# The inverse transform over 47 rows as one matrix of 96 x 94, in groups of 376 tokens

## The chip, the cores and the metric

The kernel runs on one core of one Trainium2 chip. The metric is the device time of one execution in microseconds; less is better. The engines are named as in the profile: PE is the matrix engine (PEld its weight loads), DVE, ACT and POOL work on vectors, SP issues transfers, as ACT's queue does too.

## The reference

The input x has 8 batches of 3008 rows and 256 columns, float32. The first stage goes to the frequency domain along the rows, multiplies by a complex matrix, adds a complex bias, shrinks both parts towards zero and goes back. The second is a layer pair with 256, 2048 and 256 columns on all 24,064 rows, whose weights arrive as float64.

```python
X = np.fft.rfft(x, axis=1)
Yr = Xr @ w_r - Xi @ w_i + b_r
Yi = Xr @ w_i + Xi @ w_r + b_i
Yr = np.sign(Yr) * np.maximum(np.abs(Yr) - lam, 0.0)      # Yi likewise, lam = 0.01
y = np.fft.irfft(Yr + 1j * Yi, n=3008, axis=1)
h = y.reshape(24064, 256) @ w_in
out = np.maximum(0.01 * h, h) @ w_out
```

## The kernel before

**The transform.** 3008 is 47 x 64, and the transform along the rows is done as one of 47 (index n1, frequency k1) and one of 64 (index n2, frequency k2), with the rows reordered on the host so that no factors stand between the two. As the data are real, 24 of the 47 frequencies k1 are enough. For each batch, `fwd` does the part over n1 (matrices fa), `mid` does the part over n2 (fb), the projection by w_r and w_i with bias and threshold, and the way back over k2 (gb). Between them the data lie in DRAM, in u_dram and v_dram. `mid` writes v_dram in the order (part, k1, n2, column), with part 0 the real and part 1 the imaginary one.

**The inverse over k1** is the last step and the one that is changed. v_dram has 65 places for n2, read as 5 groups of 13 (`NG`, `NS`); place 64 is padding, which `mid` fills with zeros (L334 to L336). A set is one s out of 13, with its five n2 (four for the last s). `_pairs` puts two sets together, over the border of a batch where need be: 52 pairs, most with 470 tokens. `v_load` (L478 and its neighbours) loads for each part a tile vin with 120 partitions (24 k1 x 5 groups). `inverse` runs for each half `eh` of the 256 columns: four matmuls (L499) with a slice of vin as the 120 x 128 weights and the matrix ga of 120 x 128 as the moving operand, so that the model dimension comes to lie on the partitions. The real part gives the even half of a cosine series and the imaginary part the odd half, 24 rows each. L502 (ACT) copies the odd half out of PSUM, L503 (DVE) adds for rows 0 to 23, L505 (DVE) subtracts for rows 46 down to 24, and L512 (ACT) copies the result from y into one or two chunks yc.

**The layer pair** works on 47 chunks of 512 tokens. `forms` splits a chunk into high and low fp32r halves (yh, yl) and makes the sums of a Strassen-like scheme of seven products (`forms` L524, L525 and L543 to L547). For each of eight steps q of a chunk, `moe_a` and `moe_b` do seven products of 256 columns, three matmuls each (L94, weights win); ACT and DVE add them up and apply the leaky activation (L594 to L613), `halves` splits the result into gh and gl (L577, L579), and `moe_o` multiplies by wout, 12 matmuls of 512 columns in a step (L626).

**The order.** A planner interleaves everything: while the steps of chunk ci run, `tokens(ci + 1)` advances twice in a step, 16 times in a chunk: one yield, the `v_load` of all groups whose first token lies in chunk ci + 1 (`due`), three yields, one yield for each half of each such group (`inverse`), then six yields of `forms`. `fwd` and `mid` of later batches are streams that advance in proportion. `read` says at which chunk a batch's v_dram is first needed. PSUM has two banks under the tag psf, which `inverse` shares with `fwd`, `mid` and the projection.

**Placement.** The function `placed` gives a tile some unused elements before it (`skip`) and, in the pool sb, after it (`rest`).

Of the kernel before, what the change touches and what calls it, by code (L numbers as in the profile page):

```python
# [8 lines left out]
F32 = mybir.dt.float32  # L9
# [8 lines left out]

N1, N2, NK1 = 47, 64, 24
NG, NS = 5, 13  # L20
P = 128
PA = NK1 * NG
LAMBDA = 0.01
SLOPE = 0.01

# [5 lines left out]
def spectral_mlp_kernel(  # L31
# [16 lines left out]
    nc = tc.nc  # L48
    NB = x.shape[0]
    D = w_r.shape[0]  # L50
    DF = w_in.shape[1]
    NF = DF // P
    NH = D // P
    NPAIR = NK1 // 2
    NQ = NF // 2
    NT, HT = 512, 256
    NV = 2 * NG * N1
    CS = 512
    LAG = 2
    PAUSE = 10 * CS  # L60
# [4 lines left out]
    const = ctx.enter_context(tc.tile_pool(name="const", bufs=1))  # L65
    sb = ctx.enter_context(tc.tile_pool(name="sb", bufs=2))
    dram = ctx.enter_context(tc.tile_pool(name="dram", bufs=2, space=bass.MemoryType.DRAM))
    ps = ctx.enter_context(tc.tile_pool(name="ps", bufs=1, space=bass.MemoryType.PSUM))
    sync, act, dve, pool = nc.sync, nc.scalar, nc.vector, nc.gpsimd

    def bank(tag, bufs):
        return ps.tile([P, 512], F32, name=tag, tag=tag, bufs=bufs)

# [26 lines left out]
    consts = {}  # L100
# [6 lines left out]
    def placed(pool, shape, dtype, name, skip=0, rest=0, **where):  # L107

        n = 1
        for k in shape[1:]:  # L110
            n *= k
        axes = " ".join("abcd"[:len(shape) - 1])
        t = pool.tile([shape[0], skip + n + rest], dtype, name=name, **where)[:, skip:skip + n]
        return t.rearrange(f"p ({axes}) -> p {axes}", **dict(zip("abcd", shape[1:])))
# [4 lines left out]
            for p, k in zip(("hi", "lo"), PLACE.get(name, ((0, 0), (0, 0)))))  # L119
        return consts[name]  # L120

    def load_plain(name, src, shape, skip):
        consts[name] = placed(const, shape, F32, name, skip)
        sync.dma_start(consts[name], src)

    def split_consts():
        for name in ("wr", "wd", "wn", "gb", "fa0", "fa1"):
            w = consts[name + "32"][0]
            hi, lo = pair(name, list(w.shape))
            act.copy(hi, w)  # L130
            dve.tensor_sub(lo, w, hi.bitcast(F32))

    def load_weights():

        w = sb.tile([P, 3 * NH * D + P], F32, name="w32", tag="yl")
        r, d, n = (w[:, k * NH * D:(k + 1) * NH * D].rearrange("p (a f) -> p a f", a=NH) for k in range(3))
        i = sb.tile([P, NH, D], F32, name="w_i", tag="yt", bufs=1)
        for t, src in ((r, w_r), (i, w_i)):
# [88 lines left out]
    v_dram = {}  # L227

    reads, written, turned, turning, thresholded = [], [], [], [], []
# [99 lines left out]

    def mid(b):  # L330
        ud = u_dram[b]
        vd = dram.tile([2, NK1, NG * NS, D], F32, name="v_dram", tag="v_dram")
        v_dram[b] = vd
        zero = sb.tile([2 * NK1, D], F32, name="zero", tag="kc")  # L334
        pool.memset(zero, 0.0)
        act.dma_start(vd.rearrange("c k n d -> (c k) n d")[:, N2, :], zero)  # L336
        fbt = consts["fb"]
        u_t, e_t, z_t = {}, {}, {}
        if b == 0:
# [89 lines left out]
        def stage_g(j):  # L429
            pg = bank("psh", 4) if b < 1 else bank("psf", 2)  # L430
            last = products(pg, [(consts["gb" if b else "gb32"], tuple(flat(z) for z in z_t.pop(j)))])
            if b == 0:
                turning.append(last)
            v = sb.tile([P, 2, D], F32, name="v", tag="v" if b else "y")
            act.copy(flat(v), pg)
            for c in range(2):
                act.dma_start(vd[c, 2 * j:2 * j + 2, :N2, :].rearrange("k n d -> n k d"), v[c * N2:(c + 1) * N2])

        for j in range(2):
            load(j)  # L440
# [24 lines left out]


    pairs = _pairs(NB)
    p0 = [sum(N1 * sum(n for _, _, n in c) for c in pairs[:i]) for i in range(len(pairs) + 1)]
    nch = p0[-1] // NT
    y_t, v_t, f_t, h_t, g_t, o_t = {}, {}, {}, {}, {}, {}  # L470

    def v_load(pi):
        vin = sb.tile([PA, 2, 2, D], F32, name="vin", tag="vin")
        (b, s, _), (b1, _, _) = pairs[pi]
        for c in range(2):
            if b == b1:
                vv = v_dram[b].rearrange("c k (g s) d -> c (k g) s d", g=NG)
                ld = sync.dma_start(vin[:, c, :, :], vv[c, :, s:s + 2, :])  # L478
                if pi < 2:
                    reads.append(ld)  # L480
                continue
            for i, (b_, s_, _) in enumerate(pairs[pi]):
                vv = v_dram[b_].rearrange("c k (g s) d -> c (k g) s d", g=NG)
                sync.dma_start(vin[:, c, i, :], vv[c, :, s_, :])
        v_t[pi] = vin

    def inverse(pi, eh):


        (_, _, n0), (_, _, n1) = pairs[pi]  # L490
        m = n0 + n1
        ne, n = m * NK1, m * N1
        vin = v_t[pi]
        py = bank("psf", 2)
        s = slice(eh * P, (eh + 1) * P)
        for c in range(2):
            for i in range(2):
                o = c * ne + i * n0 * NK1
                nc.tensor.matmul(py[:, o:o + P], vin[:, c, i, s], consts["ga"][:, c, :], start=True, stop=True)  # L499
        odd = sb.tile([P, 2 * NG * NK1], F32, name="odd", tag="odd", bufs=1)[:, :ne]  # L500
        y = sb.tile([P, NT], F32, name="y", tag="y")
        act.copy(odd, py[:, ne:2 * ne])  # L502
        dve.tensor_add(y[:, :ne], py[:, :ne], odd)  # L503
        ev, ov = (t.rearrange("p (m k) -> p m k", k=NK1)[:, :, 1:] for t in (py[:, :ne], odd))
        dve.tensor_sub(y[:, ne:n].rearrange("p (m k) -> p m k", m=m), ev, ov)  # L505
        lo = p0[pi]
        while lo < p0[pi + 1]:
            ci = lo // NT
            hi = min((ci + 1) * NT, p0[pi + 1])
            if ci not in f_t:  # L510
                f_t[ci] = sb.tile([P, NH, NT], F32, name="yc", tag="yc")
            act.copy(f_t[ci][:, eh, lo - ci * NT:hi - ci * NT], y[:, lo - p0[pi]:hi - p0[pi]])  # L512
            lo = hi

    def forms(ci):
# [100 lines left out]
    def moe_o(ci, q, eh):  # L616
# [19 lines left out]

    due = [[p for p in range(len(pairs)) if p0[p] // NT == ci] for ci in range(nch)]
    read = [
        max(0, min(p0[p] // NT for p, c in enumerate(pairs) if any(x[0] == b for x in c)) - 1) + 1 / (2 * NQ)
        for b in range(NB)  # L640
    ]

# [82 lines left out]
    convert_win(0)  # L725
    with tc.issue_after(turned[0].ins):
        split_consts()
    m0 = Stream(mid(0), MID)
    m0.to(0.001)
    bias = const.tile([P, 2, D], F32, name="bias")  # L730
    with tc.issue_after(reads[3].ins):
        for r, src in enumerate((b_r, b_i)):
            sync.dma_start(bias[:, r, :], src.unsqueeze(0).broadcast_to([P, D]))
    for c in range(2, 4):
        load_win(c, (sync, sync), reads[3])
    with tc.issue_after(reads[3].ins):
        load_plain("ga", ga, [PA, 2, P], 72)
    fp = Stream(fwd(1), FWD)
    with tc.issue_after(turned[0].ins):
        convert_win(1)  # L740
# [13 lines left out]
    for p in due[0]:  # L754
        v_load(p)
# [46 lines left out]
def _constants():  # L802

    import numpy as np

    n = N1 * N2

    def angles(m, rows, cols):
        j = (rows[:, None] * cols[None, :]) % m
        c, s = np.cos(2 * np.pi * j / m), np.sin(2 * np.pi * j / m)  # L810
        s[(2 * j) % m == 0] = 0.0
        return c, s

    _, half = _sequence()
    co, si = angles(N1, np.arange(NK1), np.arange(NK1))
    weight = np.where(np.arange(NK1) == 0, 1.0, 2.0)[:, None] / n
    one = np.eye(NG)
    fa = np.stack([np.kron(co, one), np.kron(-si, one)])
    ga = np.zeros((NK1, NG, 2, P))
    for c, m in enumerate((co * weight, -si * weight)):  # L820
        ga[:, :, c, :PA] = np.einsum("kn,gh->kghn", m, one).reshape(NK1, NG, PA)
    co, si = angles(N2, np.arange(N2), np.arange(N2))
    fb = np.zeros((2, N2, NK1 + 1, N2))
    fb[0, :, 0], fb[1, :, 0] = co, si
    fb[0, :, 1:] = -si[:, None, :] * half
    fb[1, :, 1:] = co[:, None, :] * half
    gb = np.block([[co, si], [-si, co]])
    f = np.float32
    return {
        "fa": fa.astype(f),  # L830
        "fb": fb.reshape(P, NK1 + 1, N2).astype(f),
        "gb": gb.astype(f),
        "ga": ga.reshape(PA, 2, P).astype(f),
        "sg": np.concatenate([
            np.concatenate([np.ones_like(half.T), half.T]),
            half.reshape(NK1 // 2, 2 * N2).T,
        ], axis=1).astype(f),
    }


def _pairs(nb):

    sets = [(b, s, NG if (NG - 1) * NS + s < N2 else NG - 1) for b in range(nb) for s in range(NS)]
    assert len(sets) % 2 == 0
    return [sets[i:i + 2] for i in range(0, len(sets), 2)]


def _tokens(nb):

    import numpy as np  # L850

    order, _ = _sequence()
    cols = []
    for c in _pairs(nb):
        n2 = [(b, NS * g + s) for b, s, n in c for g in range(n)]
        for rows in (range(NK1), range(N1 - 1, NK1 - 1, -1)):
            cols += [b * N1 * N2 + order[i, j] for b, j in n2 for i in rows]
    return np.array(cols)


# [29 lines left out]
```

## Time and profile before

| | us |
|---|---|
| median of three runs | 2549.17 |
| lowest and highest | 2546.06, 2553.24 |
| the profiled execution | 2546.58 |
| its span, first to last instruction | 2544.8 |

The page lists first the busy time of each engine over the span. The chain that ended last is followed back from the last instruction to what released each step. A group of instructions stands in one line: line of the code, engine, operation, output and inputs by the names of the program, shape and count; then busy time, mean ns of one, and the idle time of the engine before them with what ended it. Matmuls overlap, so the mean duration of one is longer than the distance from one to the next.

### The profile page before, as it was taken

The page shows a single profiled execution, that of the slowest core. Times are in us where ns is not written, and L with a number is a line of the kernel's source. Part 1 is how long each engine was busy: PE and PEld are TensorE (multiplying, and loading weights), DVE is VectorE, ACT ScalarE, POOL GpSimd, SP SyncE. Part 2 cuts the span into 40 slices and gives each one's busy share as a digit, 9 for nine tenths or more (in the row PEclk, how much of TensorE's full clock was granted, in tenths as well). Part 3 has the DMA queues.
Part 4 walks back from the last instruction along what each step waited for, and adds up shares of the span by engine and source line. Part 5 has one row for each costly group of instructions (what it writes and reads, how often), then busy time and mean ns, then how long its engine had stood idle before and what let it go on. Part 6 is the DMA issues. An engine that isn't in the chain of part 4 may idle for free.

```text
span 2544.8 us, 42449 instructions
## 1 busy us (share of the span) xinstructions
PE 2502.0 (98%) x16204; PEld 2251.4 (88%) x16204; DVE 1880.5 (74%) x3460; ACT 1675.4 (66%) x3151; POOL 119.2 (5%) x96
## 2 busy tenths in 40 slices
PE   6999999999999999999999999999999999999999
PEld 4689889999899998999989999899998998999998
DVE  7787777777877778777787677877768777666675
ACT  4777766677667765677656777567765676666564
POOL 0001000000000000000000000000000000000000
PEclk8999999999999999999999999999999999999999
DMA  8631132111321114211141111412114111100000
GB/s 269 179 94 50 43 93 86 42 50 45 105 68 46 50 37 113 59 49 50 42 114 54 50 50 38 118 54 57 39 38 130 50 54 42 45 21 29 9 17 17
DMA packets 119904, 165.12 MB, mean 65 GB/s; under 512 B 13597, under 2 KB 69909, under 8 KB 119701
## 3 DMA queue, kind: packets, MB, share of 16 engines
q1 hardware_dynamic: 79112, 115.54, 14.8%
q10 hardware_dynamic: 40589, 46.87, 7.2%
q8 instruction: 128, 2.10, 0.3%
q14 instruction: 75, 0.61, 0.1%
HBM read 86.60 MB, written 75.76 MB: 64 GB/s over the span
## 4 chain that ended last, share of the span: by engine, by line
PE 91%; DMA 3%; DVE 2%; ACT 2%; issue 1%; SPq 0%; ACTq 0%; DVEq 0%
PE pso L626 39%; PE psh L94 34%; PE psf L80 11%; PE psf L499 3%; PE psf L361 3%; DMA xin<-x_dram 1%; PE psh L80 1%; DMA u<-u_dram 1%; DMA v_dram<-v 1%; DVE gl L579 0%; DMA win_raw<-w_in_dram 0%; ACT zf L417 0%; DMA vin<-v_dram 0%; ACT zf L413 0%; PE psh L361 0%
## 5 line engine op out<-in xcount | busy, mean ns | idle before, releaser
L94 PE MATMUL psh<-yh,win_hi 128*128 128x256 f32 (+1 forms) x2608 | 736.5, 283 | 2.4 <-DVE gf L610 2.4
L94 PE MATMUL psh<-yl,win_hi 128*128 128x256 f32 (+1 forms) x2608 | 728.7, 280 | 0.0
L94 PE MATMUL psh<-yh,win_lo 128*128 128x256 f32 (+1 forms) x2608 | 726.0, 280 | 0.0
L579 DVE TENSOR_TENSOR gl<-gf,gh 128x1024 fp32r<-128x1024 f32 x376 | 461.0, 1226 | 307.1 <-ACT gh L577 297.9
L626 PE MATMUL pso<-gh,wout_hi 128*128 128x512 f32 x1504 | 590.5, 393 | 1.1 <-ACT gh L577 1.1
L626 PE MATMUL pso<-gl,wout_hi 128*128 128x512 f32 x1504 | 589.9, 392 | 1.1 <-DVE gl L579 1.1
L626 PE MATMUL pso<-gh,wout_lo 128*128 128x512 f32 x1504 | 589.3, 392 | 0.0
L94 PEld LDWEIGHTS psh<-yh,win_hi 128*128 128x128 f32 x2608 | 489.2, 188 | 19.5 <-DVE gf L610 4.8
L94 PEld LDWEIGHTS psh<-yl,win_hi 128*128 128x128 f32 x2608 | 490.5, 188 | 16.2 <-issue 0.5
L94 PEld LDWEIGHTS psh<-yh,win_lo 128*128 128x128 f32 x2608 | 489.4, 188 | 2.0
L577 ACT CAST gh<-gf 128x1024 fp32r<-128x1024 f32 x376 | 394.9, 1050 | 42.5 <-PE pso L626 31.0
L613 ACT ACTIVATE gf<-gf 128x768 f32<-128x768 f32 x368 | 311.8, 847 | 155.5 <-DVE gf L610 143.8
L626 PEld LDWEIGHTS pso<-gl,wout_hi 128*128 128x128 f32 x1504 | 282.8, 188 | 60.0 <-DVE gl L579 2.2
L626 PEld LDWEIGHTS pso<-gh,wout_hi 128*128 128x128 f32 x1504 | 283.1, 188 | 46.8 <-ACT gh L577 1.9
L626 PEld LDWEIGHTS pso<-gh,wout_lo 128*128 128x128 f32 x1504 | 282.8, 188 | 45.9 <-issue 0.2
L612 ACT ACTIVATE gf<-psh 128x256 f32<-128x256 f32 x368 | 141.7, 385 | 227.8 <-PE psh L94 219.0
L610 DVE TENSOR_TENSOR gf<-psh,u 128x512 f32<-128x512 f32 x368 | 252.1, 685 | 27.1 <-PE psh L94 25.6
L594 ACT COPY p<-psh 128x256 f32<-128x256 f32 x368 | 136.8, 372 | 153.0 <-PE psh L94 145.4
L399 POOL TENSOR_TENSOR kb<-bias,kc 128x512 f32<-128x512 f32 x84 | 116.6, 1389 | 2056.2 <-ACT kc L397 1820.9
L595 DVE TENSOR_TENSOR u<-psh,p 128x256 f32<-128x256 f32 x368 | 154.3, 419 | 70.7 <-ACT p L594 69.4
L597 DVE TENSOR_TENSOR gf<-psh,u 128x256 f32<-128x256 f32 x368 | 154.5, 420 | 29.3 <-PE psh L94 15.2
L598 DVE TENSOR_TENSOR gf<-psh,gf 128x256 f32<-128x256 f32 x368 | 154.3, 419 | 5.5
(128 smaller groups left out, 3158.9 us busy)
## 6 DMA issues: line engine op xcount, KB each, us to landing
u<-u_dram SPq DMA_DIRECT2D x192, 128.0 KB, 2.7
v_dram<-v ACTq DMA_DIRECT2D x192, 128.0 KB, 2.4
out_dram<-ob SPq DMA_DIRECT2D x94, 256.0 KB, 2.0
vin<-v_dram SPq DMA_DIRECT2D x96, 240.0 KB, 3.5
xin<-x_dram SPq DMA_DIRECT2D x90, 240.0 KB, 3.0
u_dram<-xin ACTq DMA_DIRECT2D x72, 240.0 KB, 2.4
u_dram<-xin SPq DMA_DIRECT2D x24, 240.0 KB, 4.3
raw<-w_out_dram SPq DMA_DIRECT2D x8, 512.0 KB, 4.4
```

Of the source, the lines that this page charges most:

```text
L80: last = nc.tensor.matmul(dst, a, b, start=(i == 0), stop=(i == len(terms) - 1))
L94: mlp[:] = [nc.tensor.matmul(dst, a, b, start=start and i == 0, stop=i == 2, skip_group_check=True)]
L577: cp = act.copy(gh, g)
L579: parted[:] = [cp, dve.tensor_sub(gl, g, gh.bitcast(F32))]
L594: act.copy(p1, b1[:, lo])
L595: dve.tensor_add(u2, b1[:, hi], p1)
L597: dve.tensor_add(g[:, 3], b2[:, hi], u2)
L598: dve.tensor_add(g[:, 3], b2[:, lo], g[:, 3])
L610: dve.tensor_add(g[:, 1:3], b2.rearrange("p (k n) -> p k n", k=2), u2.unsqueeze(1).broadcast_to([P, 2, HT]))
L612: act.activation(g[:, 0], b1[:, lo], AF.Prelu, alpha=SLOPE)
L613: act.activation(g[:, 1:4], g[:, 1:4], AF.Prelu, alpha=SLOPE)
L626: mlp[:] = [nc.tensor.matmul(po, a[:, f, s], r[:, i], start=(f == 0 and j == 0), stop=(f == NF - 1 and j == 2),)]
```

## The change

The inverse over k1 becomes one matrix. Real and imaginary part of a group stand together on the partitions, 2 x 24 x 2 = 96 of them (two groups of 32 n2 in place of five of 13), and the matrix ga is 96 x 94: for each of the two groups it yields all 47 rows. There is no odd half, no sum and no difference any more; ACT copies the result out of PSUM straight into yc. A group has four n2 per group of 32 (`NV` = 4), so 4 matmuls of 94 columns for each half and 376 tokens; there are 8 groups in a batch, 64 in all, and none crosses the border of a batch. v_dram has 64 places for n2 and no padding, and its zeros go. vin has 96 partitions x 4 x 256 and is loaded by one transfer. The tile bias moves from the pool const to the pool sb. The host's order of the output rows follows.

```diff
 N1, N2, NK1 = 47, 64, 24
 NG, NS = 5, 13
+NV = 4
 P = 128
 PA = NK1 * NG
+PB = NK1 * 4
...
-        vd = dram.tile([2, NK1, NG * NS, D], F32, name="v_dram", tag="v_dram")
+        vd = dram.tile([2, NK1, N2, D], F32, name="v_dram", tag="v_dram")
         v_dram[b] = vd
-        zero = sb.tile([2 * NK1, D], F32, name="zero", tag="kc")
-        pool.memset(zero, 0.0)
-        act.dma_start(vd.rearrange("c k n d -> (c k) n d")[:, N2, :], zero)
...
-    p0 = [sum(N1 * sum(n for _, _, n in c) for c in pairs[:i]) for i in range(len(pairs) + 1)]
+    p0 = [2 * N1 * NV * i for i in range(len(pairs) + 1)]
...
+        vin = sb.tile([PB, NV, D], F32, name="vin", tag="vin")
+        b, s = pairs[pi]
+        ld = sync.dma_start(vin, v_dram[b].rearrange("c k (g s) d -> (c k g) s d", g=2)[:, s:s + NV, :])
...
-        for c in range(2):
-            for i in range(2):
-                o = c * ne + i * n0 * NK1
-                nc.tensor.matmul(py[:, o:o + P], vin[:, c, i, s], consts["ga"][:, c, :], start=True, stop=True)
-        odd = sb.tile([P, 2 * NG * NK1], F32, name="odd", tag="odd", bufs=1)[:, :ne]
-        y = sb.tile([P, NT], F32, name="y", tag="y")
-        act.copy(odd, py[:, ne:2 * ne])
-        dve.tensor_add(y[:, :ne], py[:, :ne], odd)
-        ev, ov = (t.rearrange("p (m k) -> p m k", k=NK1)[:, :, 1:] for t in (py[:, :ne], odd))
-        dve.tensor_sub(y[:, ne:n].rearrange("p (m k) -> p m k", m=m), ev, ov)
+        for i in range(NV):
+            nc.tensor.matmul(py[:, i * 2 * N1:(i + 1) * 2 * N1], vin[:, i, s], consts["ga"], start=True, stop=True)
...
-            act.copy(f_t[ci][:, eh, lo - ci * NT:hi - ci * NT], y[:, lo - p0[pi]:hi - p0[pi]])
+            act.copy(f_t[ci][:, eh, lo - ci * NT:hi - ci * NT], py[:, lo - p0[pi]:hi - p0[pi]])
...
+    bias = placed(sb, [P, 2, D], F32, "bias", 0, 80, tag="bias", bufs=1)
     m0 = Stream(mid(0), MID)
     m0.to(0.001)
-    bias = const.tile([P, 2, D], F32, name="bias")
...
-        load_plain("ga", ga, [PA, 2, P], 72)
+        load_plain("ga", ga, [PB, 2 * N1], 72, 2 * P - 2 * N1)
...
-    ga = np.zeros((NK1, NG, 2, P))
-    for c, m in enumerate((co * weight, -si * weight)):
-        ga[:, :, c, :PA] = np.einsum("kn,gh->kghn", m, one).reshape(NK1, NG, PA)
+    inv = np.stack(angles(N1, np.arange(NK1), np.arange(N1))) * weight
+    ga = np.kron((inv * np.array([1.0, -1.0])[:, None, None]).reshape(2 * NK1, N1), np.eye(2))
...
-    sets = [(b, s, NG if (NG - 1) * NS + s < N2 else NG - 1) for b in range(nb) for s in range(NS)]
-    assert len(sets) % 2 == 0
-    return [sets[i:i + 2] for i in range(0, len(sets), 2)]
+    return [(b, s) for b in range(nb) for s in range(0, N2 // 2, NV)]
```

More of the change, by code (lines that the diff above doesn't have):

```diff
@@ L56, in spectral_mlp_kernel @@
     NT, HT = 512, 256
-    NV = 2 * NG * N1
     CS = 512
@@ L120, in pair, with load_plain @@
         return consts[name]
-    def load_plain(name, src, shape, skip):
-        consts[name] = placed(const, shape, F32, name, skip)
+    def load_plain(name, src, shape, skip, rest=0):
+        consts[name] = placed(const, shape, F32, name, skip, rest)
         sync.dma_start(consts[name], src)
@@ L436, in stage_g @@
             for c in range(2):
-                act.dma_start(vd[c, 2 * j:2 * j + 2, :N2, :].rearrange("k n d -> n k d"), v[c * N2:(c + 1) * N2])
+                act.dma_start(vd[c, 2 * j:2 * j + 2].rearrange("k n d -> n k d"), v[c * N2:(c + 1) * N2])
         for j in range(2):
@@ L472, in v_load @@
     def v_load(pi):
-        vin = sb.tile([PA, 2, 2, D], F32, name="vin", tag="vin")
-        (b, s, _), (b1, _, _) = pairs[pi]
-        for c in range(2):
[L476 to L484, printed above, removed]
+        vin = sb.tile([PB, NV, D], F32, name="vin", tag="vin")
+        b, s = pairs[pi]
+        ld = sync.dma_start(vin, v_dram[b].rearrange("c k (g s) d -> (c k g) s d", g=2)[:, s:s + NV, :])
+        if pi < 2:
+            reads.append(ld)
         v_t[pi] = vin
     def inverse(pi, eh):
-        (_, _, n0), (_, _, n1) = pairs[pi]
-        m = n0 + n1
-        ne, n = m * NK1, m * N1
         vin = v_t[pi]
@@ L495, in inverse @@
         s = slice(eh * P, (eh + 1) * P)
-        for c in range(2):
-            for i in range(2):
-                o = c * ne + i * n0 * NK1
-                nc.tensor.matmul(py[:, o:o + P], vin[:, c, i, s], consts["ga"][:, c, :], start=True, stop=True)
-        odd = sb.tile([P, 2 * NG * NK1], F32, name="odd", tag="odd", bufs=1)[:, :ne]
-        y = sb.tile([P, NT], F32, name="y", tag="y")
-        act.copy(odd, py[:, ne:2 * ne])
-        dve.tensor_add(y[:, :ne], py[:, :ne], odd)
-        ev, ov = (t.rearrange("p (m k) -> p m k", k=NK1)[:, :, 1:] for t in (py[:, :ne], odd))
-        dve.tensor_sub(y[:, ne:n].rearrange("p (m k) -> p m k", m=m), ev, ov)
+        for i in range(NV):
+            nc.tensor.matmul(py[:, i * 2 * N1:(i + 1) * 2 * N1], vin[:, i, s], consts["ga"], start=True, stop=True)
         lo = p0[pi]
@@ L638, in spectral_mlp_kernel @@
     read = [
-        max(0, min(p0[p] // NT for p, c in enumerate(pairs) if any(x[0] == b for x in c)) - 1) + 1 / (2 * NQ)
+        max(0, min(p0[p] // NT for p, c in enumerate(pairs) if c[0] == b) - 1) + 1 / (2 * NQ)
         for b in range(NB)
@@ L832, in _constants @@
         "gb": gb.astype(f),
-        "ga": ga.reshape(PA, 2, P).astype(f),
+        "ga": ga.astype(f),
         "sg": np.concatenate([
@@ L853, in _tokens @@
     cols = []
[L854 to L857, printed above, removed]
+    for b, s in _pairs(nb):
+        cols += [b * N1 * N2 + order[n, g * (N2 // 2) + i] for i in range(s, s + NV) for n in range(N1) for g in range(2)]
     return np.array(cols)
```

## The prediction

> **What bounds the kernel now.** I read the page's busy table first, then the chain of work that ended last, then the busy time in the stretch of the main loop.
>
> ```profile
> span 2544.8 us, 42449 instructions
> PE 2502.0 (98%) x16204; PEld 2251.4 (88%) x16204; DVE 1880.5 (74%) x3460; ACT 1675.4 (66%) x3151; POOL 119.2 (5%) x96
> ...
> PE 91%; DMA 3%; DVE 2%; ACT 2%; issue 1%; SPq 0%; ACTq 0%; DVEq 0%
> ```
>
> ```profile
> 130.00:2500.00 2370.00, 2360.61 (x15558) 2147.25 (x15557) 1758.71 (x3257) 1571.83 (x2968) 118.48 (x90) 1.00 0.20 57
> ```
>
> The columns of the second fence are the stretch, its length, then PE, PEld, DVE, ACT and POOL busy, the granted clock, the DMA share and GB/s. Between 130 and 2500 us PE is idle for 2370.00 - 2360.61 = 9.4 us, while DVE is idle for 611 us and ACT for 798 us. The granted clock is 1.00. So in this stretch the kernel lasts as long as the sequence of matmuls takes to issue, and what another engine does counts only where a matmul waits for it. The first 130 us are a start-up with its own waits; PE's busy time outside the stretch shows them, and the change touches only their end.
>
> What one matmul costs is its distance to the next, not its listed duration, because matmuls overlap. The chain in order of time shows the distance (start, length, what, and how many):
>
> ```profile
> 1041.00 2.75 PE pso L626 x12
> 1043.75 0.89 PE psf L499 x8
> 1044.65 2.42 PE psh L94 x21
> ```
>
> An L626 matmul (512 columns) takes 2.75/12 = 229 ns, an L94 matmul (256 columns) 2.42/21 = 115 ns, and an instruction of the inverse, L499, 0.89/8 = 111 ns.
>
> **The change part by part.** First the inverse on PE, the one term that stands on the path.
>
> ```profile
> L499 PE MATMUL psf<-ga,vin 120*128 120x128 f32 x832 | 112.2, 275 | 0.4 <-DVE y L505 0.4
> ```
>
> Before there are 52 groups, two halves of the model dimension each, and four matmuls in each half: 416 in the code, 832 in the row. So a plain f32 matmul is issued as two instructions, each with a weight load of its own. That makes 104 runs of eight instructions, 104 x 0.89 = 92.6 us. After it there are 64 groups, two halves, four matmuls of 94 columns: 512 in the code, 1024 instructions, 128 runs of eight. The columns fall (416 x 128 = 53,248 to 512 x 94 = 48,128, 10% less) but the instructions rise by 192 (23% more). The sum hangs on what one instruction costs when it has 94 columns instead of 128, and no matmul in the trace has so few. Two costs compete.
>
> The first is the streaming of the columns. These are loads of successive f32 matmuls of 512 columns in the start-up, where nothing but the stream limits:
>
> ```profile
> 107.28 0.18 PEld L80 LDWEIGHTS psh<-xin,fa 120*120 120x120 f32 x1 [0.25 <-issue]
> 107.71 0.18 PEld L80 LDWEIGHTS psh<-xin,fa 120*120 120x120 f32 x1 [0.25 <-issue]
> ```
>
> They are 430 ns apart, 0.84 ns a column, almost twice the 229 ns of L626, so each f32 instruction passes its columns twice. At 128 columns the stream needs 107 ns of the 111 measured; at 94 it would need 79 ns.
>
> The second is the loading of the weights. The weights of the inverse are slices of vin, 128 columns wide before and after; only their rows fall from 120 to 96. Two places in the trace show two loads in a row with no earlier matmul in the way:
>
> ```profile
> 2132.88 0.19 PEld L626 LDWEIGHTS pso<-gh,wout_hi 128*128 128x128 f32 x1 [1.49 <-ACT gh L577]
> 2132.99 0.19 PEld L626 LDWEIGHTS pso<-gh,wout_lo 128*128 128x128 f32 x1
> ```
>
> ```profile
> 2132.88 0.50 PE L626 MATMUL pso<-gh,wout_hi 128*128 128x512 f32 x1 [1.07 <-ACT gh L577]
> 2133.22 0.39 PE L626 MATMUL pso<-gh,wout_lo 128*128 128x512 f32 x1
> ```
>
> ```profile
> 360.97 0.18 PEld L80 LDWEIGHTS psf<-xz,fa_hi 120*120 120x120 f32 x1 [0.65 <-DVE xz L273]
> 361.07 0.18 PEld L80 LDWEIGHTS psf<-xz,fa_lo 120*120 120x120 f32 x1
> ```
>
> After an idle PEld the second load of 128 columns starts 110 ns behind the first, and of 120 columns 100 ns behind. In the first case the two matmuls are 340 ns apart: 110 ns for the first load and the usual 229. I read this so: a load occupies the array's weight path for some 108 ns (0.85 ns a column), a matmul starts when its load is through, and the next load starts then. Where a matmul streams for 79 ns, the next still waits for a load of 108. At 128 columns stream and load take the same time, and so the present 111 doesn't tell which of them it is.
>
> The ends are therefore 79 ns (the stream alone decides) and 111 ns (the load decides; it can't be more than now, since load and stream are both no longer than now). That is 1024 x 0.079 = 80.9, which is -11.7 us, and 1024 x 0.111 = 113.7, which is +21.1 us. With the bare 108 it is 110.6, +18.0. I take 111, because the load rows show the interval directly and the weights keep their 128 columns.
>
> The Trainium skill says in "TensorE: Matmul & The Clock Gate", section "LDWEIGHTS (loading the stationary operand)", that a load takes its columns divided by 1.2 ns, whatever its rows, 106.7 ns for 128. The pairs of loads agree (108 read from 110 and 100). By its figure alone the term would be an estimate of 109.3 us, +16.7.
>
> **ACT and DVE.** The odd copy, the sum and the difference go; the copy into yc reads PSUM.
>
> ```profile
> L512 ACT COPY yc<-y 128x470 f32<-128x470 f32 (+45 forms) x196 | 70.9, 398 | 22.7 <-DVE y L505 14.8 <-DVE y L503 5.6 <-ACT odd L502 0.9
> ...
> L435 ACT COPY v<-psf 128x512 f32<-128x512 f32 x84 | 49.0, 583 | 27.8 <-PE psf L80 25.8
> ...
> L502 ACT COPY odd<-psf 128x240 f32<-128x240 f32 (+1 forms) x104 | 36.8, 354 | 15.1 <-PE psf L499 9.7 <-PE psh L94 2.7 <-issue 1.4
> ...
> L397 ACT COPY kc<-psf 128x256 f32<-128x256 f32 x84 | 31.2, 371 | 48.8 <-PE psf L80 38.3 <-PE psh L94 9.8
> ```
>
> ```profile
> L503 DVE TENSOR_TENSOR y<-psf,odd 128x240 f32<-128x240 f32 (+1 forms) x104 | 41.4, 398 | 14.4 <-ACT odd L502 13.9
> ...
> L505 DVE TENSOR_TENSOR y<-psf,odd 128x230 f32<-128x230 f32 (+1 forms) x104 | 39.9, 383 | 0.0
> ```
>
> DVE loses 41.4 + 39.9 = 81.3 us. On ACT a copy out of PSUM costs (583 - 371)/256 = 0.83 ns a column and 159 ns beside it. The 64 groups are cut at 46 chunk borders, so there are 110 copies for each half, 220 in all, over 2 x 24,064 columns: 220 x 0.159 + 48,128 x 0.00083 = 75 us, against 70.9 + 36.8 = 107.7 before: -33 us. Neither engine is the bound. What PE can win from it is at most its idle time in the loop, 9.4 us. The two longest waits of PE there (total, times, longest) are
>
> ```profile
> PE psf L80 <- DVE xz L272: 3.1, 3, 1.3
> PE psh L94 <- DVE gf L610: 2.4, 4, 1.0
> ```
>
> for operations that remain, and the only listed wait before an L499 is 0.4 us. DVE has 4% less to do and ACT 2%, so some of these waits shorten. I take -2 us, between 0 and -9.4.
>
> **Loads and order.** vin is loaded by one transfer of 384 KB for a group instead of two of 240 KB; the zero rows, their memset and their eight transfers go, and bias sits elsewhere with the same two transfers.
>
> ```profile
> vin<-v_dram SPq DMA_DIRECT2D x96, 240.0 KB, 3.5
> ...
> raw<-w_out_dram SPq DMA_DIRECT2D x8, 512.0 KB, 4.4
> ...
> v_dram<-zero ACTq DMA_DIRECT2D x8, 48.0 KB, 1.6
> ```
>
> A transfer of 384 KB should land in some 4 us by these rows. The loads are issued several yields before the inverse, and SP's queue gets 64 in place of 112, so I count them at nothing; in the start-up, where the first L499 follows without a pause behind the L80 matmuls of batch 1, half a microsecond later costs nothing as long as those last. Two groups now fall due in 17 of the 47 chunks (64 - 47) instead of 5 (52 - 47); in such a chunk the inverse takes four yields, and the splits of forms come two later of sixteen. I count that at 0, with one split (0.7 us) late in each of the 12 added chunks as the upper end: +8.
>
> **Sum:** 2546.6 (the profiled execution: its span of 2544.8 and 1.8 around it) + 21.1 - 2 = 2565.7 us. The profiled execution lies 2.6 below the median shown, 2549.2; counted from the median it is 2568.3. I forecast 2567 us. Its own range goes from 2546.6 + 18.0 - 9.4 = 2555 to 2549.2 + 21.1 + 8 = 2578.
>
> **Rivals.**
>
> *The stream decides, and the kernel is faster.* If loads of f32 weights can run ahead by more than one matmul, an instruction costs 79 ns: -11.7 - 2, so 2533 to 2535 us. It decides at 92.6/1024 = 90 ns: below that the inverse gets cheaper. For it: the columns fall by 10%, and nothing in the trace shows a load on its own setting the pace of a long run. Against it: no two loads of 128 columns among the quoted pairs come closer than 110 ns, and L499 never needed less. Of it the Trainium skill gives, on the same page under "Back-to-back issue gap", columns divided by 2.4 plus 2.5 ns; with two passes that is an estimate of 81 ns, and the page itself says that it counts too little at few columns, as the loads are left out. The load rows speak for that reservation. Chance 0.13.
>
> *The relief pays it back.* DVE and ACT have 114 us less to do, and PE's idle time in the loop vanishes: 2546.6 + 18.0 - 9.4, and up to 3 us in the start-up, where an L499 waits for a y: 2552 to 2555 us, which is no difference that can be told. Against it: the waits quoted above end on operations that remain, and they would all have to go. Chance 0.07.
>
> *The second group comes late.* The splits of a two-group chunk reach PE after the chunk before has run out: a whole ACT cast and DVE subtraction, 0.6 + 0.7 us, in 17 chunks, +22 on top: 2588 us. Against it: five chunks had two groups before, and no wait for yh or yl stands among PE's in the loop, of which the two quoted are the longest. Chance 0.06.
>
> *It doesn't do what it says.* The compiler could issue a 94-column matmul as one instruction; then there are 512, and the inverse falls by 36 us. All plain f32 shapes in the trace are doubled, whatever their size; I give it no chance worth counting.
>
> **How the numbers follow.** Forecast 0.74, stream 0.13, relief 0.07, late group 0.06. The range of 8 in 10 runs from 2550 to 2578: it holds the forecast and most of the relief and leaves out stream and late group. A difference under 0.3% (7.6 us) can't be told from none for this kernel. Faster by more: the stream, 0.13. Within: the relief and a little of the forecast's lower end, 0.10. Slower: the rest, 0.77.
>
> **What would show it.** In the profile after: L499 x1024; runs of eight in the chain of 0.86 to 0.89 us (0.63 to 0.66 if the stream decides); no odd and no y from L503 and L505, DVE near 1800 us and ACT near 1640; PE's idle time between 130 and 2500 us still 5 to 15 us. The forecast is wrong if those runs are under 0.8 us, or if PE waits for yh, yl or vin at chunk borders.

## The result and the profile after

| | before | after |
|---|---|---|
| median of four runs, us | 2548.61 | 2563.89 |
| lowest and highest, us | 2546.06, 2553.24 | 2562.94, 2566.83 |
| profiled execution, us (its span) | 2546.58 (2544.8) | 2562.94 (2561.1) |

The ratio of after to before is 1.0063, with a 95% interval of 1.0051 to 1.0075: the changed kernel is slower by 0.6%, some 15 us.

The busy table of the kernel after, with the span above it:

```profile
span 2561.1 us, 42472 instructions
PE 2525.0 (99%) x16396; PEld 2274.1 (89%) x16396; DVE 1819.5 (71%) x3252; ACT 1644.7 (64%) x3071; POOL 114.2 (4%) x88
```

DVE is busy 61 us less and ACT 31 us less, and PE 23.0 us more, with 192 more matmuls. PE's idle time in the whole span falls from 2544.8 - 2502.0 = 42.8 us to 2561.1 - 2525.0 = 36.1. So the 16.3 us between the two spans are 23.0 more of work and 6.7 less of waiting.

The inverse's lines in the groups (busy, mean ns, idle time before):

```profile
L484 PE MATMUL psf<-ga,vin 96*128 96x94 f32 x1024 | 133.1, 271 | 0.0
...
L491 ACT COPY yc<-psf 128x376 f32<-128x376 f32 (+36 forms) x220 | 66.6, 343 | 46.7 <-PE psf L484 46.2
```

and two of its runs in the chain that ended last, in order of time (start, length, what):

```profile
1050.04 0.87 PE psf L484 x8
...
1097.98 0.86 PE psf L484 x8
```

A run of eight instructions takes 0.86 to 0.87 us in the chain, where one of the kernel before took 0.89. The chain gives a part of what a run costs to the matmul behind it. The timeline shows the whole: here is one run of the kernel before between an L626 and two L94 matmuls.

```profile
1043.37 0.39 PE L626 MATMUL pso<-gl,wout_hi 128*128 128x512 f32 x1
1043.59 1.05 PE L499 MATMUL psf<-ga,vin 120*128 120x128 f32 x8
1044.40 0.37 PE L94 MATMUL psh<-yh,win_hi 128*128 128x256 f32 x1
1044.61 0.28 PE L94 MATMUL psh<-yl,win_hi 128*128 128x256 f32 x1
```

From the end of the L626 matmul's columns (its start and 0.23 us) to the second L94, less 0.115 for the first L94, the run takes 0.90 us. A run of the changed kernel, shown under "Weights of 64 columns", takes 0.90 us as well, and inside the runs the instructions start 112 and 111 ns apart (the medians in the traces). So 94 columns cost what 128 did, some 112 ns. There are 128 runs where there were 104.

PE's waits in the loop from 130 to 2500 us are few. All that is listed (total, times, longest):

```profile
PE psh L95 <- DVE gf L589: 2.8, 4, 1.1
PE psh L95 <- DVE gf L577: 1.9, 2, 1.8
PE pso L605 <- DVE gl L558: 0.4, 1, 0.4
PE psf L81 <- DVE xz L274: 0.2, 1, 0.2
```

They add up to nearly all of PE's idle time there, 5.4 us in place of 9.4; the rest of the 6.7 us lies in the start-up and at the end. The waits for xz, 3.1 us in the row shown of before, are almost gone. No row names yh, yl or vin.

### The profile page after: what moved, and what is told of

The parts are those of the page before. It is cut to its first block, busy times and chain, and to the rows that moved or that the text cites. A ratio compares the mean times of both kernels' runs of the same rounds, so it can differ in the third digit from the quotient of the medians.

```text
span 2561.1 us, 42472 instructions
## 1 busy us (share of the span) xinstructions
PE 2525.0 (99%) x16396; PEld 2274.1 (89%) x16396; DVE 1819.5 (71%) x3252; ACT 1644.7 (64%) x3071; POOL 114.2 (4%) x88
## 4 chain that ended last, share of the span: by engine, by line
PE 91%; DMA 3%; DVE 3%; ACT 2%; issue 1%; ACTq 0%; SPq 0%; DVEq 0%
PE pso L605 38%; PE psh L95 34%; PE psf L81 11%; PE psf L484 4%; PE psf L359 3%; DMA xin<-x_dram 2%; PE psh L81 1%; DMA u_dram<-xin 1%; ACT gf L592 0%; DVE gf L589 0%; DVE gl L558 0%; ACT gh L556 0%; DMA u<-u_dram 0%; PE psh L359 0%; ACTq L435 0%
## 5 line engine op out<-in xcount | busy, mean ns | idle before, releaser
L95 PE MATMUL psh<-yh,win_hi 128*128 128x256 f32 (+1 forms) x2608 | 737.4, 283 | 4.7 <-DVE gf L589 2.8
L95 PE MATMUL psh<-yl,win_hi 128*128 128x256 f32 (+1 forms) x2608 | 729.6, 280 | 0.1
L95 PE MATMUL psh<-yh,win_lo 128*128 128x256 f32 (+1 forms) x2608 | 727.2, 280 | 0.0
L95 PEld LDWEIGHTS psh<-yh,win_hi 128*128 128x128 f32 x2608 | 489.5, 188 | 21.8 <-DVE gf L577 3.0
L95 PEld LDWEIGHTS psh<-yl,win_hi 128*128 128x128 f32 x2608 | 490.5, 188 | 16.5 <-DVE yl L504 0.6
L95 PEld LDWEIGHTS psh<-yh,win_lo 128*128 128x128 f32 x2608 | 489.8, 188 | 2.0
L592 ACT ACTIVATE gf<-gf 128x768 f32<-128x768 f32 x368 | 311.9, 848 | 186.8 <-DVE gf L589 181.3
```

The lines of the kernel that those rows point to most:

```text
L95: mlp[:] = [nc.tensor.matmul(dst, a, b, start=start and i == 0, stop=i == 2, skip_group_check=True)]
L592: act.activation(g[:, 1:4], g[:, 1:4], AF.Prelu, alpha=SLOPE)
```

## The experiments

Two questions were put: whether the weight load sets the pace of the inverse, and where the 6.7 us of shorter waiting come from. Unless another is named, a difference is taken to the kernel before on the same chip, whose medians there were 2547.8 to 2549.1 us.

### The changed kernel again

> The changed kernel once more, on the chip of the next three. Expected 2564 us, 15 us (0.6%) over the kernel before, with runs of eight inverse instructions 0.9 us apart in the chain (112 ns each).

Measured: 2561.42 us, ratio 1.0059 (1.0046 to 1.0071). This is the base for the runs that start from the changed kernel. Those with 128 columns and with the work put back ran on the same chip, four times each; 188 columns, two of 47 and weights of 64 columns were run once each, on another chip.

### What sets the pace: columns, loads, load size

**128 columns in place of 94.**

```diff
-            nc.tensor.matmul(py[:, i * 2 * N1:(i + 1) * 2 * N1], vin[:, i, s], consts["ga"], start=True, stop=True)
+            nc.tensor.matmul(py[:, i * 2 * N1:i * 2 * N1 + 128], vin[:, i, s], consts["ga"], start=True, stop=True)
...
```

The host's padding of ga and its load change with it.

> The changed kernel with its matrix padded with zeros from 94 to 128 columns; each matmul writes over the junk of the one before. Weight loads and their number stay. Load theory (a load of 128 columns sets 112 ns for each instruction): no change, 2564 us, 2561 to 2567. Stream theory (the columns set the pace): 34 columns more at 0.84 ns for 1024 instructions, +29 us, 2593 us.

Measured: 2565.03 us, 3.6 more than the changed kernel. A run in its chain of 1040 to 1100 us:

```profile
1056.36 0.89 PE psf L484 x8
```

That is 3 ns an instruction more than in the chain of the changed kernel; 1024 x 3 ns is 3 us, not the 29 of the stream theory. Measured between the full matmuls around it, a run of eight takes 0.90 us here too, so even these 3 us aren't the columns'. (Profiles of single runs differ by as much elsewhere: between 330 and 430 us PE is idle for 3.9 us in this one and 0.3 in that of the changed kernel in the run above.) A quarter fewer columns bring nothing that can be told.

**188 columns.** The same edit with 188 for 128.

> The changed kernel with its matrix padded to 188 columns, so that the stream (188 x 0.84 = 158 ns) is longer than a load. Load theory: the pace passes to the stream, 158 ns each, 1024 x 46 ns = +47 us, 2611 us. A theory of a fixed cost of 112 ns beside the stream would give +79 us (94 x 0.84 x 1024) on the changed kernel, 2643 us.

Measured: 2615.98 us. Two of its runs in the chain:

```profile
1054.13 0.64 PE psf L484 x4
...
1073.37 1.28 PE psf L484 x8
```

1.28/8 = 160 ns, where 158 were expected from the stream alone. So the costs don't add: the longer of load and stream counts. (The 0.64 us of four give the same 160.)

**Two matmuls of 47 columns, each with its own load of the same weights.**

```diff
-            nc.tensor.matmul(py[:, i * 2 * N1:(i + 1) * 2 * N1], vin[:, i, s], consts["ga"], start=True, stop=True)
+            for h in range(2):
+                o = h * N1
+                nc.tensor.matmul(
+                    py[:, i * 2 * N1 + o:i * 2 * N1 + o + N1], vin[:, i, s], consts["ga"][:, o:o + N1],
+                    start=True, stop=True)
```

> The changed kernel with each matmul of 94 columns cut into two of 47, with the same weights loaded for each: the columns in all stay, the loads double to 2048. Load theory: 1024 more at 112 ns, +115 us, 2679 us. Stream theory: 39 ns each, nothing changes in the total, at most 2564 us.

Measured: 2674.78 us, 113 more than the changed kernel.

```profile
1043.09 1.72 PE psf L486 x16
```

The columns in all are the same and the runs are twice as long: 1.72 us for 16 in the chain and 1.79 between the full matmuls, 108 and 112 ns each, though the stream of 47 columns would need 39.

**Weights of 64 columns.**

```diff
-            nc.tensor.matmul(py[:, i * 2 * N1:(i + 1) * 2 * N1], vin[:, i, s], consts["ga"], start=True, stop=True)
+            for h in range(2):
+                r = slice(eh * P + 64 * h, eh * P + 64 * h + 64)
+                nc.tensor.matmul(
+                    py[64 * h:64 * h + 64, i * 2 * N1:(i + 1) * 2 * N1], vin[:, i, r], consts["ga"],
+                    start=True, stop=True)
```

> The changed kernel with each matmul cut into two that take 64 columns of vin as weights each: 2048 instructions again, each with 94 columns to stream but a load of half the size (54 ns at 0.85 ns a column). Load theory: the stream of 79 ns decides, 2048 x 0.080 = 164 in place of 115 us, +49 us, 2613 us. Fixed-cost theory (112 ns an instruction, whatever it loads): +115 us, 2679 us, as for two of 47.

Measured: 2585.67 us, 24 more than the changed kernel. The fixed-cost theory is out (115), and the load theory's number is missed by half, to the fast side. One run on PE, in the timeline (start, length to the last end, what):

```profile
797.09 0.40 PE L609 MATMUL pso<-gl,wout_hi 128*128 128x512 f32 x1
797.41 0.87 PE L486 MATMUL psf<-ga,vin 96*64 96x94 f32 x16
798.21 0.39 PE L95 MATMUL psh<-yh,win_hi 128*128 128x256 f32 x1
798.43 0.28 PE L95 MATMUL psh<-yl,win_hi 128*128 128x256 f32 x1
```

and one of the changed kernel, between the same neighbours:

```profile
1049.65 0.39 PE L605 MATMUL pso<-gl,wout_hi 128*128 128x512 f32 x1
1049.87 1.03 PE L484 MATMUL psf<-ga,vin 96*128 96x94 f32 x8
1050.69 0.36 PE L95 MATMUL psh<-yh,win_hi 128*128 128x256 f32 x1
1050.89 0.28 PE L95 MATMUL psh<-yl,win_hi 128*128 128x256 f32 x1
```

From its first to its last end a run of sixteen takes 0.87 us, less than the 1.03 of eight with 128-column weights. Matmuls on the two halves of the array's columns run beside each other: the pairs start 81 ns apart in the trace, so a pair costs about one stream, not two. What is lost is at the ends. From the last full matmul's columns (its start and 0.23 us) to the second L95, less 0.115 for the first, it is 1.00 us with the narrow weights and 0.90 with the wide ones. Measured in this way in the trace, a run of sixteen takes a median of 1.00 us, one of four still 0.51 and one of two 0.50, so some 0.35 us go with each run, however short; the wide ones take 0.90, 0.45 and 0.23. All runs after 130 us come to 135.3 us against 111.7: the 24 us. That the change of width is what costs the 0.35 us was not tried by itself.

Together the four runs answer the first question. With weights of 128 columns an f32 instruction takes some 112 ns at 47, 94 and 128 columns, and at 188 its stream of 160 ns: the longer of load and stream. A cost for each instruction that doesn't depend on the load is out, since with weights of 64 columns the pairs follow at the pace of the stream.

### What the lighter ACT and DVE gave

**The kernel before with the light eviction.**

```diff
-        odd = sb.tile([P, 2 * NG * NK1], F32, name="odd", tag="odd", bufs=1)[:, :ne]
-        y = sb.tile([P, NT], F32, name="y", tag="y")
-        act.copy(odd, py[:, ne:2 * ne])
-        dve.tensor_add(y[:, :ne], py[:, :ne], odd)
-        ev, ov = (t.rearrange("p (m k) -> p m k", k=NK1)[:, :, 1:] for t in (py[:, :ne], odd))
-        dve.tensor_sub(y[:, ne:n].rearrange("p (m k) -> p m k", m=m), ev, ov)
...
-            act.copy(f_t[ci][:, eh, lo - ci * NT:hi - ci * NT], y[:, lo - p0[pi]:hi - p0[pi]])
+            act.copy(f_t[ci][:, eh, lo - ci * NT:hi - ci * NT], py[:, lo - p0[pi]:hi - p0[pi]])
```

> The kernel before without the odd copy, the sum and the difference (left out: the output lacks the recombination); ACT copies the matmul's result straight from PSUM to yc. PE's instructions are those of the kernel before. Relief theory (the lighter ACT and DVE are what took some 6 us from PE's idle time in the changed kernel): 2548.6 - 6 = 2543 us, 2540 to 2545, PE idle near 36 us. Rival (the idle time fell by the new groups and order, or by chance of one profile): 2548 us, PE idle near 43 us.

Measured: 2542.94 us, ratio 0.9981 (0.9972 to 0.9990): -4.9 us. The relief is real and near the size that the balance of the two profiles asks for. PE's idle time in its profile, the slowest of its runs, is 40.2 us, not the 36 expected.

**The changed kernel with the work put back.**

```diff
+        ne = 2 * NG * NK1
+        odd = sb.tile([P, 2 * NG * NK1], F32, name="odd", tag="odd", bufs=1)
+        y = sb.tile([P, NT], F32, name="y", tag="y")
+        act.copy(odd[:, :188], py[:, :188])
+        dve.tensor_add(y[:, :188], py[:, 188:376], odd[:, :188])
+        dve.tensor_sub(y[:, 188:376], py[:, 188:376], odd[:, :188])
         lo = p0[pi]
```

> The changed kernel with an odd copy, a sum and a difference of 188 columns put back for each half of each group, to scratch tiles that nobody reads (+41 us on ACT and +84 us on DVE by the rows of before). Relief theory: +6 us on the changed kernel, 2570 us, 2567 to 2573. Rival: no change, 2564 us.

Measured: 2578.35 us, ratio 1.0122 (1.0108 to 1.0136), 16.9 more than the changed kernel: the right sign, and almost three times the size. Its profile says where. In the following rows, all of the view of busy time by stretch, the columns are the stretch, its length, then PE, PEld, DVE, ACT and POOL busy with their counts, the granted clock, DMA share and GB/s. First the changed kernel in the run above, then the one with the work put back:

```profile
130.00:530.00 400.00, 399.66 (x2607) 361.49 (x2607) 292.25 (x527) 268.37 (x518) 25.78 (x18) 1.00 0.24 67
530.00:2500.00 1970.00, 1965.65 (x13056) 1794.46 (x13055) 1398.70 (x2517) 1268.08 (x2365) 88.14 (x66) 1.00 0.19 55
```

```profile
130.00:530.00 400.00, 392.11 (x2479) 350.99 (x2479) 293.71 (x548) 263.19 (x513) 24.40 (x17) 0.98 0.23 66
530.00:2500.00 1970.00, 1967.19 (x13085) 1796.22 (x13084) 1449.12 (x2725) 1300.13 (x2482) 93.01 (x67) 1.00 0.20 55
```

By 530 us PE has done 128 instructions fewer; at 2370/15,660 = 0.151 us each that is 19 us, more than the whole difference. After 530 us it is not behind. PE is idle for 7.9 us before 530 in place of 0.3, and the granted clock is 0.98 instead of 1.00, which is some 8 us of 400: the two together are about the difference. The longest waits between 230 and 430 us are for ACT's eh and ob, and then for xz (total, times, longest):

```profile
PE psf L81 <- ACT eh L375: 2.9, 1, 2.9
PE pso L611 <- ACT ob L616: 2.8, 1, 2.8
PE psf L81 <- DVE xz L273: 1.8, 2, 1.0
```

In the timeline of that run PE goes at half speed for a while:

```profile
378.46 0.63 PE L611 MATMUL pso<-gh,wout_hi 128*128 128x512 f32 x1
378.89 0.63 PE L611 MATMUL pso<-gh,wout_lo 128*128 128x512 f32 x1
```

These start 0.43 us apart, where 0.23 is usual. The kernel before has the same fault, only shorter:

```profile
361.54 1.07 PE L499 MATMUL psf<-ga,vin 120*128 120x128 f32 x8
363.87 0.47 PE L80 MATMUL psf<-xz,fa_hi 120*120 120x512 f32 x1 [1.27 <-DVE xz L272]
...
366.00 0.63 PE L626 MATMUL pso<-gl,wout_hi 128*128 128x512 f32 x1
366.43 0.63 PE L626 MATMUL pso<-gh,wout_hi 128*128 128x512 f32 x1
```

At 357 to 365 us the forward stream of batch 2 begins. PE waits for its splits xz, which DVE makes late (for one of them, before 362 us, DVE itself waits 1.1 us for the transfer of xin), and afterwards PE runs at half the clock for about 3 us. Before that, at 303 us, stands one more wait, for ACT (total, times, longest):

```profile
PE psf L80 <- ACT eh L377: 1.5, 1, 1.5
```

From this came a theory of the place: the relief is not spread over the run but sits where this stream begins.

**The light eviction early, and late.** The edit of the kernel before, once for its first 10 pairs (shown) and once for the other 42 (with `pi <= 9`):

```diff
+        if pi > 9:
             odd = sb.tile([P, 2 * NG * NK1], F32, name="odd", tag="odd", bufs=1)[:, :ne]
...
+        else:
+            y = py
```

> The kernel before, with the odd copy, the sum and the difference left out for the first 10 of its 52 pairs alone (their tokens lack the recombination), those that are done before some 520 us. Theory of the place (the relief is the waits and the halved clock between 250 and 430 us, where the stream of the next batch begins): the whole relief, -5 us on the kernel before, with no fall of the clock between 330 and 430 us. Rival (the relief is spread over the run, in proportion to the work left out): 10/52 of 5 = -1 us.

Measured: 2540.79 us, ratio 0.9970 (0.9960 to 0.9980): -7.0 us.

> The counterpart: the odd copy, the sum and the difference left out for the last 42 pairs alone, kept for the first 10. Theory of the place: no change against the kernel before (-1 to +1 us), with the waits near 357 us still there. Rival: 42/52 of 5 = -4 us.

Measured: 2550.40 us, ratio 1.0010 (1.0001 to 1.0018): +2.6 us. The stretch from 330 to 430 us of the kernel before, of the early and of the late edit:

```profile
330.00:430.00 100.00, 96.25 (x602) 85.05 (x600) 81.06 (x154) 61.33 (x117) 3.52 (x2) 0.98 0.36 104
```

```profile
330.00:430.00 100.00, 99.41 (x635) 89.31 (x636) 80.05 (x149) 64.65 (x120) 2.58 (x2) 1.00 0.36 104
```

```profile
330.00:430.00 100.00, 97.50 (x601) 86.23 (x601) 80.64 (x153) 63.08 (x120) 3.52 (x2) 0.97 0.36 104
```

The early edit does 33 instructions more in these 100 us, at a full clock; the late one is as the kernel before. Between 230 and 430 us the early edit's profile lists no wait for xz or eh any more. The place theory holds: 10 of 52 pairs bring more than all of them. The edit takes work and a step of the chain from ACT and DVE at once, and it changes when a bank of PSUM comes free; which of these counts was not tried. The two parts add up, -7.0 + 2.6 = -4.4 against the -4.9 of both. Why the light eviction costs 2.6 us later is not settled: PE waits longer there for gf, 4.0 us in place of 2.4 in the profiles from 530 us on, and the planner's order differs; no run tells these apart.

**The complete kernel before, with the stream's start moved.**

```diff
-        yield 4 * CS if b >= NPRE else 0
+        yield 8 * CS if b >= NPRE else 0
...
-            streams = ([Stream(fwd(cur + 1), FWD + 4 * CS)] if cur else []) + [mids[cur]]
+            streams = ([Stream(fwd(cur + 1), FWD + 8 * CS)] if cur else []) + [mids[cur]]
```

> The kernel before, complete, with one number changed: a later batch's forward stream waits twice as long between its first loads and its first fold (8 x CS in place of 4 x CS of planned work). Theory of the place: the splits xz of batch 2 reach PE in time, the waits near 357 us and the half clock behind them go: -4 us on the kernel before, 2544 us. Rival (the wait follows the stream wherever it is put): no change.

Measured: 2545.31 us, ratio 0.9983 (0.9974 to 0.9993): -3.4 us, so this version beats both kernels.

> As the run before, with 12 x CS. Theory of the place: as with 8, -4 us, 2544 us; rival: no change or, as the rest of the stream has less time, slower by a few us.

Measured: 2548.86 us, ratio 1.0003 (0.9994 to 1.0012): nothing, where -4 us was expected. The same stretch, with 8 and with 12:

```profile
330.00:430.00 100.00, 97.52 (x620) 87.02 (x620) 79.33 (x152) 61.42 (x116) 2.11 (x3) 1.00 0.38 107
```

```profile
330.00:430.00 100.00, 97.00 (x596) 86.07 (x596) 76.42 (x146) 60.51 (x114) 3.27 (x3) 0.97 0.38 107
```

PE's idle time in the stretch is alike, 2.5 and 3.0 us, but with 8 the clock stays at 1.00 and with 12 it falls. The gain with 8 is the clock that wasn't lost and 1.3 us less of waiting, as far as this stretch goes. The theory of the place expected the waits to go, and they went only in part: between 230 and 430 us a wait of 1.0 us for xz is left with 8. With 12 none for xz is listed, but 2.5 us for the transfer of vin before L499 stand in its place; no run shows why that transfer is late.

The traces also allow a division by place. The first L626 (or its counterpart) of a chunk stands for the same progress of the layer pair in every version; chunks are counted from 0. The times between these marks in the profiled executions, in us:

| | start to chunk 1 | chunk 1 to 6 | chunk 6 to 46 | chunk 46 to the end |
|---|---|---|---|---|
| kernel before | 182.3 | 284.6 | 2037.7 | 40.2 |
| light eviction | 186.1 | 277.2 | 2040.4 | 40.2 |
| light early | 183.0 | 277.1 | 2038.4 | 40.1 |
| light late | 181.3 | 284.5 | 2041.3 | 40.2 |
| start at 8 x CS | 185.7 | 280.9 | 2036.0 | 40.2 |
| start at 12 x CS | 185.5 | 284.9 | 2038.3 | 40.2 |
| changed kernel | 184.9 | 281.8 | 2054.7 | 39.7 |
| work put back | 185.9 | 297.1 | 2053.6 | 39.7 |

Between chunks 1 and 6 the light eviction and its early form win over 7 us and the late form nothing; later, from chunk 6 to 46, both that are light there lose some 3 us. The work put back costs 15 us in the same place and nothing behind it. The first column scatters by 4.4 us even among the four versions whose edits begin only behind chunk 1 (kernel before, light late, 8 and 12 x CS).

## Why the prediction was right, point by point

**The inverse on PE** was right in its mechanism and size. The load interval, read from two pairs of loads, decides; four runs with other columns, other numbers of loads and other sizes of weights bear it out. By the chain the forecast of 111 ns for an instruction came out at 108, 128 x 0.865 - 92.6 = +18 us on the term, but the chain leaves a part of a run to its successor. By the distances between the full matmuls around a run, 0.90 us before and after, it is 24 x 0.90 = +21.6, where +21.1 was forecast. The marks agree: from chunk 6 to 46 there are 160 instructions more, 160 x 0.112 = 17.9 us, and the changed kernel takes 17.0 longer. The Trainium skill's figure for a load, 106.7 ns ("TensorE: Matmul & The Clock Gate", "LDWEIGHTS (loading the stationary operand)"), is below the 112 ns in the traces: its estimate of +16.7 falls some 5 us short.

**The stream rival** (79 ns, faster) is refuted by the profile alone: 0.86 us a run, where it needed 0.63. **The relief rival** is out too, with 2563.9 us in place of 2552 to 2555: PE's idle time in the loop fell to 5.4 us and didn't vanish. The 3 us that this rival took for the start-up had no row behind them; the wait listed before an L499 there is 0.4 us.

**The relief of ACT and DVE** was the term that was mis-sized: -2 us was taken, within 0 to -9.4, and it is -5 (the light eviction in the kernel before). What failed is the step that shared the relief out by load, 4% and 2% less on engines that aren't the bound. The waits sit in one place, and the clock that falls behind them makes PE's own work longer, which idle time doesn't show. So idle time wasn't a sound bound, though the relief stayed within its 9.4 us: putting the work back cost 16.9, about half of it by the clock. With -5 in place of -2 the sum would have been 2562.7 us for the profiled execution, which took 2562.9. That it comes so near is partly luck. By the marks the changed kernel gains more between chunks 1 and 6, 2.8 us in spite of 32 instructions more (3.6 us), which makes 6.4; and it loses 2.6 in the start-up, which the prediction put at nothing and which lies within the spread of the first column.

**The busy times off the path.** ACT at 1644.7 and DVE at 1819.5 came out as forecast in the last step of the prediction. The 81 us that L503 and L505 were given are a sum of single lines; DVE's busy time fell by 61, since the page counts overlapping stretches once: in the trace of before, only 60 us of DVE's busy time belong to these two lines alone.

**Loads and order** cost nothing, as forecast: 384 KB landed in 3.6 us, and the second group in 17 chunks made no wait for yh or yl.

**The range** of 2550 to 2578 us holds 2563.9. The forecast of 2567 is 3 us above it, as much as the relief brought beyond the 2 us taken.

## What to carry to other kernels

Where a matmul streams for less time than its successor's weights take to load, count loads, not columns: this change saved 10% of the columns, added 23% to the loads, and the loads decided. Take the cost of a short run of matmuls between the full matmuls around it, since the chain shifts a part of it to the next line. Work taken off an engine that isn't the bound is worth what the bound engine waits for it at particular places, so look for these in the timeline rather than spread the saving over the run. A few waits close together can cost more than their length, because the clock can fall behind them.

## What the runs showed of the hardware

- **Half clock after a handful of short waits.** In the kernel before, PE waited 1.3 us at most at a time between 357 and 365 us, with matmuls between, some 3.7 us in all, and then ran 512-column matmuls 0.43 us apart in place of 0.23 for about 3 us. Waits don't always do it: with the stream's start at 8 x CS, PE was idle for 2.5 us between 330 and 430 us and the granted clock stayed at 1.00. The Trainium skill, "TensorE: Matmul & The Clock Gate", section "Part 1: The HAM clock gate", has half rate after one idle window of about 3.4 us; the half rate agrees, but here no single wait is that long.
- **Two column halves at once.** With 64-column weights 16 instructions of 94 columns stood 0.80 us in the timeline, against 1.72 us for 16 of 47 columns with 128-column weights. The Trainium skill, "TensorE: Matmul & The Clock Gate", section "Part 3: Packing small matmuls — row/col tiling", says that small matmuls on different tiles of the array run at the same time; this trace agrees. Some 0.35 us were lost around each such run.
